# Causal attention on another grid: query chunks of 64 and three times 128, key blocks of 128, with 64x64 corners

## The chip, the cores and the metric

The program runs on one core of one Trainium2 chip. The metric is the device time of the whole program in microseconds (us), the median of three runs. One more execution was recorded by the hardware profiler, and everything below that speaks of engines and waits is read from it.

## What is computed

A causal attention over 2 batches of 12 heads (448 tokens, head size 64), then two MLPs on its 896 x 768 output, the first gated. The weights come as 64-bit floats.

```python
scores = q @ k.T / sqrt(64), masked above the diagonal     # per head, 448 x 448
attn = exp(scores - rowmax); attn /= sum + 1e-9
x = (attn @ v) with the heads side by side                  # 896 x 768
x = (silu(x @ w_gate) * (x @ w_val)) @ w_out                # 768 -> 1536 -> 768
h = x @ w_in                                                # 768 -> 2048
out = (h * clip(h + 3, 0, 6) / 6) @ w2_out                  # 2048 -> 768
```

## The kernel before

The heads are worked in 12 pairs. A pair's q and k lie transposed, head size on the partitions, one head on partitions 0 to 63 and the other on 64 to 127; each is split into a high and a low fp32r part (`qh`, `ql`, `kh`, `kl`). A head's queries and its keys are both cut into four chunks of 112 (`C`, `NC`). Five steps make one pair:

- `sc_parts`: for each chunk c of queries and each head, the three products qh.kh, qh.kl and ql.kh into a PSUM bank (`sc`), 112 rows by (c + 1) x 112 keys (224 at least). A head's contraction is 64 long, so the two heads stand on the two halves of the array's rows and run at the same time. Then VectorE adds the mask and takes the row's maximum (one custom instruction for each chunk, with a read of its accumulator), and ScalarE takes the exponential with its row sum (likewise), into `e`.
- `tp_parts`: TensorE turns every 112x112 block of `e` on or below the diagonal, 20 a pair; six bank copies on ScalarE or VectorE bring them to `et`.
- `pv_parts`, `product`: for each block of keys, `v` (112 x 64, plain f32) times `et`, both heads at the same time on the two halves of the array's columns. An f32 matmul leaves two records in the trace.
- `shares`: the reciprocals of the row sums are spread over 64 columns on GpSimd (`rb`) and turned by TensorE (`tr`), four 112 x 128 transposes.
- `last`: `pv` times the turned reciprocals, and the split of the result for the MLP.

Around them: transfers of q, k and v on SP's queue, turning of q and k (on VectorE from the third pair on, on TensorE for the first two), and near the end the first six-matmul pieces of the MLP (`mm`).

Steps of three pairs are under way at once: at step t the plan is given the scores of pair t, the products with v of pair t - 2 and the transposes of pair t - 1, in this order (`order`). Each step is an `op` with a cost per engine that can take it; `Plan.run` then sets the order on every engine by due times and these costs, and all instructions of the attention are issued from line 74, so that the profile names one line for all and tiles tell them apart. The MLPs behind the attention have a plan of their own, which the change leaves alone.

Of the kernel before, what the change touches and what calls it, by code (L numbers as in the profile page):

```python
# [21 lines left out]
EB = 4  # L22
# [36 lines left out]
GROUPS = ((2,), (0, 1), (3,))  # L59
# [156 lines left out]
def tile_attention_glu_mlp(  # L216
# [38 lines left out]
    OFF = [0, C, 3 * C, 6 * C]  # L255
    KOFF = [0, 4 * C, 7 * C, 9 * C]
    EW = 10 * C
# [77 lines left out]
    def attention():  # L335
        with ExitStack() as st:
# [6 lines left out]
            mask = fix.tile([C, S], F32, name="mask")  # L343
            nc.gpsimd.memset(mask, 0.0)
            nc.gpsimd.affine_select(
                out=mask[:, S - C :], in_=mask[:, S - C :], pattern=[[-1, C]],
                compare_op=ALU.is_ge, fill=LOW, base=0, channel_multiplier=1,
            )
            vset = []
            for i in range(NV):  # L350
                t = fix.tile([C, 2, NC, D + 16], F32, name=f"v1_{i}")
                vset.append(t)
# [183 lines left out]
            def sc_parts(p):  # L536

                if p >= NPAIR:
                    return []
                qh, ql, kh, kl = sets(p)  # L540
                es = e_of[p] = [take("e", EB, [C, EW]) for _ in range(2)]
                ms = [take("m", EB, [C, NC]) for _ in range(2)]
                sm = s_of[p] = take("s", 3, [C, 2, NC])

                def products(group):
                    got = [bank("sc") for _ in range(2)]
                    o, places = 0, {}
                    for c in group:
                        places[c] = o, max(2, c + 1) * C
                        o += places[c][1]  # L550

                    terms = ((qh, kh), (qh, kl), (ql, kh))

                    def work(eng, cs, terms_):
                        for c in cs:
                            o, w = places[c]
# [16 lines left out]
                    for j, (sp, bn) in enumerate(got):  # L573
                        e, m = es[j], ms[j]
                        for x in group:
                            at, w = places[x][0], (x + 1) * C
                            cols_ = slice(OFF[x], OFF[x] + w)
                            op(
                                {"vec": 0.09 + w * 0.00101},
                                lambda eng, x=x, at=at, w=w, cols_=cols_, e=e, m=m, sp=sp: eng.tensor_tensor_reduce(  # L580
                                    out=e()[:, cols_], in0=sp()[:C, at : at + w], in1=mask[:, S - w :], op0=ALU.add,
                                    op1=ALU.min, scale=-SCALE, scalar=3.0e38, accum_out=m()[:, x : x + 1],
                                ),
                                reads=[sp], writes=[(e, x), (m, x)],
                            )
                            op(
                                {"act": 0.28 + w * 0.00083},
                                lambda eng, x=x, cols_=cols_, e=e, m=m, j=j: eng.activation(
                                    out=e()[:, cols_], in_=e()[:, cols_], func=AF.Exp, scale=-1.0, bias=m()[:, x : x + 1],
                                    accum_out=sm()[:, j, x : x + 1],  # L590
                                ),
                                reads=[(m, x)], writes=[(e, x), (sm, (j, x))],
                            )
                        idle.append(bn)

                return [lambda g=g: products(g) for g in GROUPS]

            def tp_parts(p):

                if p < 0 or p >= NPAIR:  # L600
                    return []
                es = e_of.pop(p)
                ets = et_of[p] = [take("et", TB, [C, EW]) for _ in range(2)]

                def turns(j, ks):
# [14 lines left out]
                    n *= C  # L620
                    op(
                        {"act": 0.03 + n * 0.00095, "vec": 0.09 + n * 0.001},
                        lambda eng: move(eng, et()[:, lo : lo + n], tp()[:C, :n]), reads=[tp],
                        writes=[(et, kc) for kc in ks],
                    )
                    idle.append(bn)

                return [lambda j=j, ks=ks: turns(j, ks) for ks in ((0,), (1,), (2, 3)) for j in range(2)]

            def pv_parts(p):  # L630
# [7 lines left out]
                def product(kc):  # L638
                    if kc == 0:
                        box["o"], box["n"] = bank("pv")  # L640
                    o, w = box["o"], (NC - kc) * C

                    def work(eng):
                        for j, et in enumerate(ets):
                            eng.matmul(
                                o()[64 * j : 64 * j + 64, kc * C : S], vt()[:, j, kc, :D], et()[:, KOFF[kc] : KOFF[kc] + w],
                                start=(kc == 0), stop=(kc == NC - 1),
                            )

                    op({"pe": w * 0.0018}, work, reads=[(et, kc) for et in ets] + [vt], writes=[o], kind="pv")  # L650

                def shares():
                    r, rb = take("r", 2, [C, 2, NC]), take("rb", 1, [C, NC, 2, D])
# [9 lines left out]
                        {"pool": 0.72},  # L663
                        lambda e: e.tensor_copy(
                            rb(), r().rearrange("p j c -> p c j").unsqueeze(3).to_broadcast([C, NC, 2, D])
                        ),
# [13 lines left out]
                def last():  # L680
# [961 lines left out]
```

## Time and profile before

| | us |
|---|---|
| median of three runs | 542.94 (541.97 to 543.34) |
| the profiled execution | 542.55 |
| its span, first to last instruction | 540.8 |
| PE / DVE / ACT / POOL busy | 534.3 / 455.9 / 418.6 / 146.2 |

PE is TensorE, PEld its loading of stationary operands, DVE VectorE, ACT ScalarE, POOL GpSimd, SP the queue that issues transfers. The granted clock of TensorE is the full one in all 40 slices of the span. The ends of matmuls in the trace are modelled; their starts are measured, so that a matmul's cost is read from the distance of starts, or from the chain, which counts each piece from the end of the one before. The attention fills the first 92 us.

### The profile page before, as it was taken

To read this page: it belongs to the slowest core of one execution; us is meant where nothing else is said; L and a number is where in the kernel's file an instruction comes from. 1 tells how busy PE (TensorE), PEld (TensorE's weight loads), DVE (VectorE), ACT (ScalarE), POOL (GpSimd) and SP (SyncE) were. 2 spreads that over 40 slices of the span, in tenths; PEclk is the share of its full clock that TensorE was granted. 3 is DMA by queue.
4 is the path that set the end of the run, shared out by engine and by line. 5 is a ranking of instruction groups with operands and counts; after the bars stand their busy time and mean duration, and the time that the engine had idled before them with its cause. 6 is when DMAs were issued, how large, how long until landed. Compare 5 with 4: busy or idle time off the path is not lost.

```text
span 540.8 us, 8943 instructions
## 1 busy us (share of the span) xinstructions
PE 534.3 (99%) x3099; PEld 487.6 (90%) x3099; DVE 455.9 (84%) x931; ACT 418.6 (77%) x877; POOL 146.2 (27%) x163
## 2 busy tenths in 40 slices
PE   8999999999999999999999999999999999999997
PEld 4777777999999999999999999999999999999997
DVE  4999997999878778688998888989888956599982
ACT  5999996878887678588967788899898756686560
POOL 0798988403000000030030143322231300000311
PEclk9999999999999999999999999999999999999999
DMA  7987803355545443332002354465353155510112
GB/s 204 245 215 201 170 17 118 117 180 191 182 148 181 134 135 135 118 116 79 1 1 78 110 176 135 127 185 166 117 163 130 35 180 195 176 58 2 59 45 102
DMA packets 58989, 69.32 MB, mean 128 GB/s; under 512 B 16960, under 2 KB 52544, under 8 KB 58944
## 3 DMA queue, kind: packets, MB, share of 16 engines
q1 hardware_dynamic: 58944, 68.76, 42.4%
q8 instruction: 24, 0.39, 0.3%
q14 instruction: 21, 0.17, 0.1%
HBM read 65.99 MB, written 2.75 MB: 127 GB/s over the span
## 4 chain that ended last, share of the span: by engine, by line
PE 98%; DVE 1%; ACT 0%; issue 0%
PE mm L74 83%; PE pv L74 5%; PE sc L74 4%; PE tp L74 4%; PE tr L74 2%; PE zero L74 1%; DVE out L74 0%; ACT e L74 0%; DVE et L74 0%; ACT qh L74 0%; DVE e L74 0%; DVE zeros L341 0%; DVE half L840 0%; DVE half L839 0%; DVE m L74 0%
## 5 line engine op out<-in xcount | busy, mean ns | idle before, releaser
L74 PE MATMUL mm<-x,a 128*128 128x448 f32 x396 | 85.9, 363 | 0.0
L74 PE MATMUL mm<-x,s 128*128 128x448 f32 x378 | 80.6, 363 | 0.0
L74 PEld LDWEIGHTS mm<-x,a 128*128 128x128 f32 x396 | 74.6, 189 | 5.3
L74 PEld LDWEIGHTS mm<-x,s 128*128 128x128 f32 x378 | 71.2, 188 | 5.1
L74 ACT ACTIVATE raw<-raw,half 128x768 uint32<-128x768 uint8 (+1 forms) x66 | 64.5, 981 | 0.0
L74 PE MATMUL mm<-t,s 128*128 128x448 f32 x270 | 57.8, 363 | 0.0
L74 PE MATMUL mm<-op 128*128 128x384 f32 x315 | 56.5, 336 | 0.0
L74 PEld LDWEIGHTS mm<-op 128*128 128x128 f32 x315 | 55.1, 188 | 0.0
L74 PEld LDWEIGHTS mm<-t,s 128*128 128x128 f32 x270 | 50.7, 188 | 3.7
L74 PE MATMUL mm<-go,wo 128*128 128x448 f32 x252 | 51.2, 363 | 0.0
L74 PEld LDWEIGHTS mm<-go,wo 128*128 128x128 f32 x252 | 47.4, 188 | 3.5 <-issue 0.2
L74 ACT ACTIVATE e<-e,m 112x224 f32<-112x224 f32 (+3 forms) x96 | 49.7, 535 | 0.6 <-DVE m L74 0.6
L74 DVE CUSTOM_DVE_ANT_0 e<-sc,mask 112x224 f32<-112x224 f32 (+3 forms) x96 | 36.6, 440 | 1.2 <-PE sc L74 1.1
L74 DVE SCALAR_TENSOR_TENSOR v<-v,raw 128x768 uint32<-128x768 uint32 x36 | 34.3, 954 | 2.7 <-ACT raw L74 2.4
L74 ACT ACTIVATE w<-raw 128x768 f32<-128x768 f32 (+1 forms) x34 | 29.6, 870 | 8.6 <-DMA raw<-in_moe_w_out_dram 4.3
L74 ACT ACTIVATE v<-raw 128x768 f32<-128x768 f32 x36 | 32.5, 907 | 1.2 <-DMA raw<-in_moe_w_val_dram 1.0
L74 PE MATMUL mm<-x,ws 128*128 128x448 f32 x144 | 30.1, 366 | 0.0
L74 DVE SCALAR_TENSOR_TENSOR w<-w,raw 128x768 uint32<-128x768 uint32 (+1 forms) x30 | 27.2, 906 | 3.0 <-ACT raw L74 3.0
L74 PEld LDWEIGHTS mm<-x,ws 128*128 128x128 f32 x144 | 26.8, 188 | 2.2
L74 ACT COPY tmp<-mm 128x448 f32<-128x448 f32 x40 | 21.2, 532 | 9.0 <-PE mm L74 8.8
L74 ACT CAST op<-h 128x384 fp32r<-128x384 f32 x30 | 15.3, 511 | 16.2 <-PE mm L74 15.5
L74 PE MATMUL tp<-keep,e 112*112 112x112 f32 x240 | 25.8, 260 | 1.4 <-ACT e L74 1.4
(252 smaller groups left out, 1253.6 us busy)
## 6 DMA issues: line engine op xcount, KB each, us to landing
raw<-in_moe_w_out_dram SPq DMA_DIRECT2D x24, 768.0 KB, 4.2
raw<-in_moe_w_in_dram SPq DMA_DIRECT2D x16, 768.0 KB, 4.5
raw<-in_moe_w_gate_dram SPq DMA_DIRECT2D x12, 768.0 KB, 4.2
raw<-in_moe_w_val_dram SPq DMA_DIRECT2D x12, 768.0 KB, 4.2
raw<-in_moe_w_out_dram SPq DMA_DIRECT2D x6, 512.0 KB, 3.4
v<-in_v_dram SPq DMA_DIRECT2D x12, 224.0 KB, 5.1
out_dram<-out SPq DMA_DIRECT2D x14, 192.0 KB, 1.9
nat<-in_k_dram SPq DMA_DIRECT2D x10, 216.0 KB, 4.9
```

Of the source, the lines that this page charges most:

```text
L74: ins = call(*args, **kw)
```

## The change

Queries of a head are cut into chunks of 64, 128, 128 and 128 (`ROWS`), keys into blocks of 128, 128, 128 and 64. Chunk c needs exactly 64, 192, 320 or 448 keys (`WIDE`), and the last block of a chunk's keys is a corner of 64. The chunks of 64 of both heads lie in one tile of 128 partitions, so that the mask, the maximum, the exponential and the row sums take seven passes a pair instead of eight, 1984 columns instead of 2240. Scores go to four banks a pair instead of six, the turned blocks to four instead of six. The products for the chunk of 64 are made in plain f32 with 64 stationary columns. Of `e`, twelve full 128x128 blocks, one 128x64 and six 64x64 corners are turned; `product` has three steps (a 64x64 block, three full ones, three corners); `shares` turns three full blocks and makes two 64x64 products. `v` comes in three transfers a pair instead of one. The plan gets costs for the new pieces.

```diff
...
-GROUPS = ((2,), (0, 1), (3,))
+GROUPS = ((0, 3), (1, 2))
+SMALL, TURN, HALF_TURN, HALF_PV = 0.1, 0.1125, 0.06, 0.13
...
-    OFF = [0, C, 3 * C, 6 * C]
-    KOFF = [0, 4 * C, 7 * C, 9 * C]
-    EW = 10 * C
+    R = S // 7
+    ROWS = [(0, R), (R, 2 * R), (3 * R, 2 * R), (5 * R, 2 * R)]
+    WIDE = [a + n for a, n in ROWS]
+    OFF = [15 * R, 0, 3 * R, 8 * R]
+    EW = 16 * R
+    LONG, MID = ((0, 1), (0, 2), (0, 3), (2, 3)), ((1, 2), (1, 3))
+    HB = 8 * R
...
+            for o, w, r in ((S - 2 * R, 2 * R, slice(0, 128)), (S, R, slice(0, 64)), (S, R, slice(64, 128))):
+                nc.gpsimd.affine_select(
+                    out=mask[r, o : o + w], in_=mask[r, o : o + w], pattern=[[-1, w]],
+                    compare_op=ALU.is_ge, fill=LOW, base=0, channel_multiplier=1,
+                )
...
+                for j in range(2):
+                    op(
+                        {"sp": 0.5},
+                        lambda e, j=j: e.dma_start(
+                            out=vt()[:, j, :3, :D],
+                            in_=v[b, 2 * hp + j, : 6 * R].rearrange("(c p) d -> p c d", p=128),
+                        ),
+                        writes=[(vt, j)], wire=0.43, soon=SOON,
+                    )
                 op(
                     {"sp": 0.5},
                     lambda e: e.dma_start(
-                        out=vt().rearrange("p j c d -> p (j c) d")[:, :, :D],
-                        in_=v[b, 2 * hp : 2 * hp + 2].rearrange("j (c p) d -> p (j c) d", p=C),
+                        out=vt()[:R, :, 3, :D], in_=v[b, 2 * hp : 2 * hp + 2, 6 * R :].rearrange("j p d -> p j d"),
                     ),
-                    writes=[vt], wire=1.0, soon=SOON,
+                    writes=[(vt, 2)], wire=0.15, soon=SOON,
                 )
...
+                        places[c] = o
+                        o += WIDE[c]
...
+                            o, w, (at, n) = places[c], WIDE[c], ROWS[c]
+                            kind = (lambda x: x) if c else (lambda x: x.bitcast(F32))
                             for i in terms_:
                                 a, b = terms[i]
                                 for j, (sp, _) in enumerate(got):
                                     r = slice(64 * j, 64 * j + 64)
+                                    t = sp()[:, o : o + w] if c else got[0][0]()[r, o : o + w]
                                     eng.matmul(
-                                        sp()[:C, o : o + w], a()[r, c * C : (c + 1) * C], b()[r, :w],
-                                        start=(i == 0), stop=(i == 2),
+                                        t, kind(a()[r, at : at + n]), kind(b()[r, :w]), start=(i == 0), stop=(i == 2),
                                     )
...
                     for cs, terms_ in steps:
                         op(
-                            {"pe": len(terms_) * sum(0.005 + places[c][1] * 0.00044 for c in cs)},
+                            {"pe": len(terms_) * sum(max(SMALL, 0.005 + WIDE[c] * 0.00044) if c else HALF_PV for c in cs)},
                             lambda eng, cs=cs, terms_=terms_: work(eng, cs, terms_),
                             reads=[x for i in terms_ for x in terms[i]], writes=[sp for sp, _ in got], kind="sc",
                         )
...
+                            if x == 0 and j:
+                                continue
+                            at, w, n = places[x], WIDE[x], 2 * (x - 1) + j if x else 6
                             cols_ = slice(OFF[x], OFF[x] + w)
+                            low = slice(S - w, S) if x else slice(S, S + R)
...
+                                    out=e()[:, cols_], in0=sp()[:, at : at + w], in1=mask[:, low], op0=ALU.add,
+                                    op1=ALU.min, scale=-SCALE, scalar=3.0e38, accum_out=ms()[:, n : n + 1],
                                 ),
-                                reads=[sp], writes=[(e, x), (m, x)],
+                                reads=[sp], writes=[(e, x), (ms, n)],
...
+                                    out=e()[:, cols_], in_=e()[:, cols_], func=AF.Exp, scale=-1.0, bias=ms()[:, n : n + 1],
+                                    accum_out=sm()[:, n : n + 1],
                                 ),
-                                reads=[(m, x)], writes=[(e, x), (sm, (j, x))],
+                                reads=[(ms, n)], writes=[(e, x), (sm, n)],
...
-                ets = et_of[p] = [take("et", TB, [C, EW]) for _ in range(2)]
-
-                def turns(j, ks):
+                ets = et_of[p] = [take("et", TB, [128, EW]) for _ in range(2)]
+
+                def turns(b):
                     tp, bn = bank("tp")
-                    e, et, lo = es[j], ets[j], KOFF[ks[0]]
+                    et, lo = ets[b // 2], b % 2 * HB
+                    rows, low = slice(0, R if b == 3 else 128), slice(64, 128)
 
                     def work(eng):
-                        for kc in ks:
-                            for c in range(kc, NC):
-                                to = KOFF[kc] - lo + (c - kc) * C
-                                at = OFF[c] + kc * C
-                                eng.transpose(tp()[:C, to : to + C], e()[:, at : at + C], ident[:C, :C])
-
-                    n = sum(NC - kc for kc in ks)
+                        if b == 3:
+                            eng.transpose(tp()[:R, : 2 * R], es[0]()[:, OFF[0] : OFF[0] + R], ident)
+                            for i in range(6):
+                                e, c = es[i // 3], i % 3 + 1
+                                at = OFF[c] + WIDE[c] - R
+                                eng.transpose(
+                                    tp()[:R, (i + 2) * R : (i + 3) * R], e()[low, at : at + R], ident[low, low]
+                                )
+                            return
+                        for i, (j, kc, c) in enumerate(
+                            [(j, *x) for j in range(2) for x in MID] if b == 2 else [(b, *x) for x in LONG]
+                        ):
+                            at = OFF[c] + kc * 128
+                            eng.transpose(tp()[:, i * 128 : (i + 1) * 128], es[j]()[:, at : at + 128], ident)
+
+                    need = [(es[j], c) for j in ((b,) if b < 2 else (0, 1)) for c in ((2, 3) if b == 2 else (1, 2, 3))]
                     op(
-                        {"pe": 0.098 * n}, work, reads=[(e, c) for c in range(ks[0], NC)], writes=[tp], kind="tp",
-                    )
-                    n *= C
+                        {"pe": TURN + 6 * HALF_TURN if b == 3 else 4 * TURN}, work,
+                        reads=need + [(es[0], 0)] * (b == 3), writes=[tp], kind="tp",
+                    )
                     op(
-                        {"act": 0.03 + n * 0.00095, "vec": 0.09 + n * 0.001},
-                        lambda eng: move(eng, et()[:, lo : lo + n], tp()[:C, :n]), reads=[tp],
-                        writes=[(et, kc) for kc in ks],
+                        {"act": 0.03 + HB * 0.00095, "vec": 0.09 + HB * 0.001},
+                        lambda eng: move(eng, et()[rows, lo : lo + HB], tp()[rows]), reads=[tp], writes=[(et, b % 2)],
                     )
                     idle.append(bn)
 
-                return [lambda j=j, ks=ks: turns(j, ks) for ks in ((0,), (1,), (2, 3)) for j in range(2)]
+                return [lambda b=b: turns(b) for b in (0, 1, 3, 2)]
...
-                def product(kc):
-                    if kc == 0:
+                def product(g):
+                    if g == 0:
                         box["o"], box["n"] = bank("pv")
-                    o, w = box["o"], (NC - kc) * C
+                    o = box["o"]
+                    full, low = slice(0, 128), slice(0, 64)
+                    runs = (
+                        (
+                            (low, 0, 0, R, (HB, HB + R), 1), (full, 0, R, 6 * R, (0, HB), 0),
+                            (full, 2, 5 * R, 2 * R, (6 * R, HB + 6 * R), 0),
+                        ),
+                        ((full, 1, 3 * R, 4 * R, (0, 4 * R), 1),),
+                        tuple((low, c, 2 * R * c, R, (HB + (c + 1) * R, HB + (c + 4) * R), 1) for c in (1, 2, 3)),
+                    )[g]
 
                     def work(eng):
-                        for j, et in enumerate(ets):
-                            eng.matmul(
-                                o()[64 * j : 64 * j + 64, kc * C : S], vt()[:, j, kc, :D], et()[:, KOFF[kc] : KOFF[kc] + w],
-                                start=(kc == 0), stop=(kc == NC - 1),
-                            )
-
-                    op({"pe": w * 0.0018}, work, reads=[(et, kc) for et in ets] + [vt], writes=[o], kind="pv")
+                        for rows, kc, to, w, at, i in runs:
+                            for j in range(2):
+                                eng.matmul(
+                                    o()[64 * j : 64 * j + 64, to : to + w], vt()[rows, j, kc, :D],
+                                    ets[i]()[rows, at[j] : at[j] + w], start=kc == 0, stop=True, skip_group_check=True,
+                                )
+
+                    op(
+                        {"pe": sum(HALF_PV if x[3] == R else x[3] * 0.0018 for x in runs)}, work,
+                        reads=[vt] + ([(ets[0], 0), (ets[0], 1), (ets[1], 1)], [(ets[1], 0)], [(ets[1], 1)])[g],
+                        writes=[o], kind="pv",
+                    )
...
                     def work(eng):
-                        for c in range(NC):
+                        for i in range(3):
                             eng.transpose(
-                                tr()[:, c * C : (c + 1) * C], rb()[:, c].rearrange("p j d -> p (j d)"), ident[:C, :C]
+                                tr()[:, R + i * 128 : R + (i + 1) * 128],
+                                rb()[:, 2 * i : 2 * i + 2].rearrange("p j d -> p (j d)"), ident,
                             )
-
-                    op({"pe": 0.4}, work, reads=[rb], writes=[tr], kind="tp")
+                        for j in range(2):
+                            h = slice(64 * j, 64 * j + 64)
+                            eng.matmul(tr()[h, :R], rb()[h, 6], ident[h, h], start=True, stop=True, skip_group_check=True)
+
+                    op({"pe": 3 * TURN + HALF_PV}, work, reads=[rb], writes=[tr], kind="tp")
...
-                return [lambda kc=kc: product(kc) for kc in range(2)] + [shares] + [
-                    lambda kc=kc: product(kc) for kc in range(2, NC)
-                ] + [last]
+                return [lambda: product(0), shares, lambda: product(1), lambda: product(2), last]
...
```

The next two places show PE's own order in the middle of the attention, where the plan repeats it from pair to pair. A row gives the tile written, the tiles read, the size of the output (partitions x columns) and how often the row stands in succession. First, PE from the transposes of one pair (`tp`) into the scores of another (`sc`), before:

```order
L74 MATMUL tp<-keep,e 112x112 x20
L74 MATMUL sc<-kh,qh 112x336 x2
L74 MATMUL sc<-kl,qh 112x336 x2
L74 MATMUL sc<-kh,ql 112x336 x2
L74 MATMUL sc<-kh,qh 112x224 x2
```

and now:

```order
L75 MATMUL tp<-keep,e 128x128 x4
L75 MATMUL sc<-kh,qh 64x64 x2
L75 MATMUL sc<-kl,qh 64x64 x2
L75 MATMUL sc<-kh,ql 64x64 x2
L75 MATMUL sc<-kh,qh 128x448 x2
L75 MATMUL sc<-kl,qh 128x448 x2
```

Between the transposes and the scores with 128 rows now stand the products of the chunk of 64, with 64 rows and 64 columns; the widths 336, 224, 224, 448 became 448, 192 and 320.

Second, PE from the products with v (`pv`) over the turned reciprocals (`tr`) and the transposes (`tp`) to the next scores (`v` with a number is one of its four buffers), before:

```order
L74 MATMUL pv<-et,v_3_95 64x448 x2
L74 MATMUL pv<-et,v_3_95 64x336 x2
L74 MATMUL pv<-et,v_3_95 64x224 x2
L74 MATMUL pv<-et,v_3_95 64x112 x2
L74 MATMUL tr<-keep,rb 128x112 x4
L74 MATMUL tp<-keep,e 112x112 x20
L74 MATMUL sc<-kh,qh 112x336 x2
```

and now:

```order
L75 MATMUL pv<-et,v_2_100 64x64 x2
L75 MATMUL pv<-et,v_2_100 64x384 x2
L75 MATMUL pv<-et,v_2_100 64x128 x2
L75 MATMUL pv<-et,v_2_100 64x256 x2
L75 MATMUL pv<-et,v_2_100 64x64 x6
L75 MATMUL tr<-keep,rb 128x128 x3
L75 MATMUL tr<-keep,rb 64x64 x2
L75 MATMUL tp<-keep,e 128x128 x8
L75 MATMUL tp<-keep,e 64x128
L75 MATMUL tp<-keep,e 64x64 x6
L75 MATMUL tp<-keep,e 128x128 x4
L75 MATMUL sc<-kh,qh 64x64 x2
```

One run of `pv` with 112 keys each, one of `tr` and one of `tp` became: `pv` with 64, with 128 and again with 64 keys; `tr` as three full transposes and two 64x64 products; `tp` as eight full, one with 64 stationary columns, six 64x64 and four full transposes.

## Rows read from the trace of the kernel before

**Rows 1.** The page, busy time and its share of the span, with the number of instructions.

```profile
PE 534.3 (99%) x3099; PEld 487.6 (90%) x3099; DVE 455.9 (84%) x931; ACT 418.6 (77%) x877; POOL 146.2 (27%) x163
```

**Rows 2.** Waits of PE, whole execution: engine, line, waited for: us in total, times, longest.

```profile
PE tp L74 <- ACT e L74: 1.4, 1, 1.4
PE zero L74 <- DVE half L840: 1.2, 1, 1.2
PE sc L74 <- DVE m L74: 0.3, 1, 0.3
```

**Rows 3.** Busy us (instructions) per engine, clock, DMA; seven pairs, one a stretch.

```profile
30.50:36.87 6.37, 6.37 (x65) 4.89 (x64) 6.34 (x24) 6.37 (x25) 5.58 (x9) 1.00 0.97 247
...
68.73:75.11 6.38, 6.38 (x66) 4.90 (x66) 6.26 (x23) 6.31 (x21) 6.15 (x9) 1.00 0.00 0
sum 44.61, PE 44.61 PEld 34.29 DVE 43.47 ACT 44.01 POOL 40.36; mean PE 6.37 PEld 4.90 DVE 6.21 ACT 6.29 POOL 5.77
```

**Rows 4.** The chain, one pair: start us, us, engine, tile, records.

```profile
30.57 1.88 PE sc L74 x24
32.45 2.04 PE pv L74 x16
34.49 0.54 PE tr L74 x4
35.02 1.92 PE tp L74 x20
```

**Rows 5.** The chain, earlier, where v products stand in two pieces.

```profile
17.53 0.90 PE pv L74 x4
...
20.32 1.29 PE pv L74 x12
```

**Rows 6.** The chain, end of the attention: mm is the first MLP matmul.

```profile
83.99 1.41 PE mm L74 x6
85.41 0.38 PE tr L74 x4
85.79 0.77 PE tp L74 x8
86.56 1.23 PE mm L74 x6
```

**Rows 7.** Timeline of PE, one pair's scores: start us, us, stationary partitions*columns, moving operand.

```profile
30.50 0.41 PE L74 MATMUL sc<-kh,qh 64*112 64x336 f32 x2
30.75 0.32 PE L74 MATMUL sc<-kl,qh 64*112 64x336 f32 x2
30.90 0.32 PE L74 MATMUL sc<-kh,ql 64*112 64x336 f32 x2
31.06 0.27 PE L74 MATMUL sc<-kh,qh 64*112 64x224 f32 x2
...
31.68 0.37 PE L74 MATMUL sc<-kh,qh 64*112 64x448 f32 x2
31.88 0.36 PE L74 MATMUL sc<-kl,qh 64*112 64x448 f32 x2
32.09 0.37 PE L74 MATMUL sc<-kh,ql 64*112 64x448 f32 x2
32.38 2.11 PE L74 MATMUL pv<-et,v 112*64 112x448 f32 x16
```

**Rows 8.** Timeline of PE, first transposes of pair 0.

```profile
12.94 0.79 PE L74 MATMUL tp<-keep,e 112*112 112x112 f32 x6 [1.43 <-ACT e L74]
```

**Rows 9.** Timeline, an issue on SP's queue.

```profile
34.17 0.41 SPq L74 DMA_DIRECT2D nat<-in_k_dram  x1
```

**Rows 10.** Groups of instructions by form: busy us, mean ns, idle before; POOL's mask pass.

```profile
L345 POOL TENSOR_SCALAR_AFFINE_SELECT mask<-mask 112x112 f32<-112x112 f32 x1 | 0.3, 278 | 0.0
```

More of the change, by code (lines that the diff above doesn't have):

```diff
@@ L342, in attention @@
             make_identity(nc, ident)
-            mask = fix.tile([C, S], F32, name="mask")
+            mask = fix.tile([128, S + R], F32, name="mask")
             nc.gpsimd.memset(mask, 0.0)
-            nc.gpsimd.affine_select(
-                out=mask[:, S - C :], in_=mask[:, S - C :], pattern=[[-1, C]],
-                compare_op=ALU.is_ge, fill=LOW, base=0, channel_multiplier=1,
-            )
+            for o, w, r in ((S - 2 * R, 2 * R, slice(0, 128)), (S, R, slice(0, 64)), (S, R, slice(64, 128))):
[3 more added lines that the diff above has]
+                )
             vset = []
             for i in range(NV):
-                t = fix.tile([C, 2, NC, D + 16], F32, name=f"v1_{i}")
+                t = fix.tile([128, 2, 4, D + 16], F32, name=f"v1_{i}")
                 vset.append(t)
@@ L540, in sc_parts @@
                 qh, ql, kh, kl = sets(p)
-                es = e_of[p] = [take("e", EB, [C, EW]) for _ in range(2)]
-                ms = [take("m", EB, [C, NC]) for _ in range(2)]
-                sm = s_of[p] = take("s", 3, [C, 2, NC])
+                es = e_of[p] = [take("e", EB, [128, EW]) for _ in range(2)]
+                ms = take("m", 2, [128, 7])
+                sm = s_of[p] = take("s", 3, [128, 7])
                 def products(group):
@@ L548, in products @@
                     for c in group:
-                        places[c] = o, max(2, c + 1) * C
-                        o += places[c][1]
+                        places[c] = o
+                        o += WIDE[c]
                     terms = ((qh, kh), (qh, kl), (ql, kh))
@@ L555, in work @@
                         for c in cs:
-                            o, w = places[c]
+                            o, w, (at, n) = places[c], WIDE[c], ROWS[c]
+                            kind = (lambda x: x) if c else (lambda x: x.bitcast(F32))
                             for i in terms_:
@@ L573, in products @@
                     for j, (sp, bn) in enumerate(got):
-                        e, m = es[j], ms[j]
+                        e = es[j]
                         for x in group:
-                            at, w = places[x][0], (x + 1) * C
+                            if x == 0 and j:
+                                continue
+                            at, w, n = places[x], WIDE[x], 2 * (x - 1) + j if x else 6
                             cols_ = slice(OFF[x], OFF[x] + w)
+                            low = slice(S - w, S) if x else slice(S, S + R)
                             op(
                                 {"vec": 0.09 + w * 0.00101},
-                                lambda eng, x=x, at=at, w=w, cols_=cols_, e=e, m=m, sp=sp: eng.tensor_tensor_reduce(
-                                    out=e()[:, cols_], in0=sp()[:C, at : at + w], in1=mask[:, S - w :], op0=ALU.add,
-                                    op1=ALU.min, scale=-SCALE, scalar=3.0e38, accum_out=m()[:, x : x + 1],
+                                lambda eng, n=n, at=at, w=w, cols_=cols_, e=e, sp=sp, low=low: eng.tensor_tensor_reduce(
+                                    out=e()[:, cols_], in0=sp()[:, at : at + w], in1=mask[:, low], op0=ALU.add,
+                                    op1=ALU.min, scale=-SCALE, scalar=3.0e38, accum_out=ms()[:, n : n + 1],
                                 ),
-                                reads=[sp], writes=[(e, x), (m, x)],
+                                reads=[sp], writes=[(e, x), (ms, n)],
                             )
@@ L587, in products @@
                                 {"act": 0.28 + w * 0.00083},
-                                lambda eng, x=x, cols_=cols_, e=e, m=m, j=j: eng.activation(
-                                    out=e()[:, cols_], in_=e()[:, cols_], func=AF.Exp, scale=-1.0, bias=m()[:, x : x + 1],
-                                    accum_out=sm()[:, j, x : x + 1],
+                                lambda eng, n=n, cols_=cols_, e=e: eng.activation(
+                                    out=e()[:, cols_], in_=e()[:, cols_], func=AF.Exp, scale=-1.0, bias=ms()[:, n : n + 1],
+                                    accum_out=sm()[:, n : n + 1],
                                 ),
-                                reads=[(m, x)], writes=[(e, x), (sm, (j, x))],
+                                reads=[(ms, n)], writes=[(e, x), (sm, n)],
                             )
@@ L636, in pv_parts @@
                 box = {}
-                def product(kc):
-                    if kc == 0:
+                def product(g):
+                    if g == 0:
                         box["o"], box["n"] = bank("pv")
-                    o, w = box["o"], (NC - kc) * C
-                    def work(eng):
-                        for j, et in enumerate(ets):
-                            eng.matmul(
-                                o()[64 * j : 64 * j + 64, kc * C : S], vt()[:, j, kc, :D], et()[:, KOFF[kc] : KOFF[kc] + w],
-                                start=(kc == 0), stop=(kc == NC - 1),
-                            )
-                    op({"pe": w * 0.0018}, work, reads=[(et, kc) for et in ets] + [vt], writes=[o], kind="pv")
+                    o = box["o"]
[8 more added lines that the diff above has]
+                    )[g]
+                    def work(eng):
+                        for rows, kc, to, w, at, i in runs:
[9 more added lines that the diff above has]
+                    )
                 def shares():
-                    r, rb = take("r", 2, [C, 2, NC]), take("rb", 1, [C, NC, 2, D])
+                    r, rb = take("r", 2, [128, 7]), take("rb", 1, [128, 7, D])
                     tr, bn = bank("tr")
@@ L662, in shares @@
                     op(
[L663 to L666, printed above, removed]
+                        {"pool": 0.63},
+                        lambda e: e.tensor_copy(rb(), r().unsqueeze(2).to_broadcast([128, 7, D])),
                         reads=[r], writes=[rb], port=True,
```

## The prediction

> **What bounds the kernel now.** I went from the page to the waits, then to the chain, then to single matmuls. The page has TensorE (PE) busy for 534.3 of 540.8 us [rows 1]; a busy PE can still be a waiting one, so the list of its waits comes next: over the whole execution it waited 1.4 us once for a softmax result, 1.2 us at the very start and 0.3 us once [rows 2]. Everything else is PE running one matmul behind the other. The change touches only the attention, the first 92 us. There seven head pairs in a row take 6.36 to 6.38 us each; of those 6.37 us PE is busy all 6.37, ScalarE (ACT) 6.29 and VectorE (DVE) 6.21 [rows 3]. Three engines look full, and the question is which sets the period. A period set by ACT or DVE would show PE gaps; there are none. So an instruction saved on ACT or DVE is worth nothing here, and PE's time per pair is worth twelve times itself, since PE has no slack behind the attention either.
>
> The chain splits a period: scores 1.88, products with v 2.04, spreading of the reciprocals 0.54, transposes 1.92, in all 6.38 [rows 4]. What these contain is the second thing to read. A matmul uses the whole array, half of its rows (at most 64 partitions of contraction), half of its columns (at most 64 stationary columns), or a quarter. The same work costs more when the piece before it had another shape:
> - four `tr` transposes take 0.54 after `pv` (half columns to whole array) [rows 4], and 0.38 after `mm` (whole to whole) [rows 6]: 0.16 for the change of shape;
> - the sixteen `pv` records take 2.04 in one piece [rows 4], and 0.90 + 1.29 = 2.19 where the scores of the next pair were put between them [rows 5]: 0.15 for one more entry;
> - six `mm` take 1.41 after `pv` and 1.23 after `tp` [rows 6]: 0.18;
> - scores: steps of 0.155 at 336 columns, 0.62 for six of 224, 0.205 at 448 [rows 7], so 3 x 0.155 + 0.62 + 3 x 0.205 = 1.70 for the matmuls, and 1.88 - 1.70 = 0.18 for entering from the transposes.
>
> Another data type alone costs nothing: `mm` (fp32r) and the f32 transposes follow each other on the whole array without it [rows 6]. A pair of before has three changes of shape (into sc, pv, tr): 0.18 + 0.15 + 0.16 = 0.49, and 5.89 us of matmuls.
>
> **The change part by part.** *Matmuls.* Scores: three terms at 448 columns stay 0.615; 320 columns lie between 224 and 336, by proportion 0.148, three are 0.44; 192 columns lie between 0.088 (by columns from 448) and 0.103 (the 224 step), I take 0.10, three are 0.30; the shared 64 chunk runs in plain f32 on quarters, both heads side by side. Its price comes from `pv`, f32 too: 2.04 - 0.15 = 1.89 us for 448 + 336 + 224 + 112 = 1120 columns, 1.69 ns a column, 0.108 for 64, three are 0.32. Sum 1.68 against 1.70. `pv`: 384 + 128 + 256 + 4 x 64 = 1024 columns, 1.73 against 1.89. `tp`: 1.92 / 20 = 0.096 for 112 columns [rows 4], so 0.110 for 128 and 0.055 for 64; thirteen with 128 and six with 64 make 1.76 against 1.92. `tr`: 3 x 0.110 + 0.108 = 0.44 against 0.38. In all 5.61 against 5.89: 0.28 less a pair, **-3.4 us** for twelve. Rounding in these proportions leaves 1 us to either side.
>
> *Changes of shape.* A pair of after goes: quarter, half rows (scores); quarter, half columns, quarter (pv); whole, quarter (tr); whole, half columns, quarter, whole (tp). That is eleven changes for three. Over the whole program, counted in its order, 135 for 47: 88 more. No row of before shows a quarter of the array, so the price there is bounded by the four above, 0.15 to 0.18, above, and by nothing at all, below. The dear two load 112 or 128 fp32r columns after the change, the cheap ones 64 columns or transposes; the new ones are nearly all 64 wide or transposes. I take the nearest row, 0.15: 88 x 0.15 = **+13.2 us**. At 0.12 it is 10.6, at 0.18 it is 15.8.
>
> The Trainium skill (TensorEngine Tiling (Array Packing), Key Properties) says that a change of tiling mode, not of the tile alone, drains TensorE. The rows above show drains for four pairs of shapes; the rule would make every one of the 88 pay, quarters included, and so stands with the +13.2 and not with the first two rivals below.
>
> *ACT and DVE.* Seven exponentials and seven max passes a pair instead of eight, four bank copies instead of six, 1984 and 2048 columns instead of 2240: both get lighter, below a period that they don't set, and I count 0. Where it can count is the start, before the pipeline is full: the first transposes of pair 0 wait 1.43 us for their exponentials [rows 8]. The new first transposes need three chunks of one head, behind four exponentials on ACT where the old ones stood behind five. All of it gone is -1.4, none of it, with the new entries in the first scores, +0.5; I take **-0.5**.
>
> *SP, POOL, DMA.* v comes in three transfers for one, two more issues of 0.41 us a pair on SP's queue [rows 9], for the same bytes, ahead of the next q and k; PE waited for no transfer anywhere [rows 2], and with a longer period there is more room. Two more mask passes of at most 0.28 us on POOL [rows 10] end before the first scores. Both 0; if v came late, `pv` of pair 0 would wait once, well under 1 us.
>
> *Sum:* 13.2 - 3.4 - 0.5 = +9.3 on the profiled execution's 542.55: 551.9. That execution lies 0.4 under the median 542.94, so **552** against the median.
>
> **The rivals.**
> - *Only entering or leaving the whole array costs* (a quarter is reached from a half for nothing). 74 such changes for 36, +38 x 0.15 = 5.7, less 3.9: +1.8, 544.7. For it: no row shows a quarter. Against it: scores to pv is half rows to half columns, and pays 0.15.
> - *The price belongs to the change of step, not of shape*, so changes inside a step are free: 0 - 3.4 - 0.5, **539.0**, faster. It decides from the point where the mean price of the added changes falls below 3.9 / 88 = 0.044. For it: in before each change of shape is also one of step. Against it: tr to tp, tp to mm and mm to tr are changes of step too, and their 0.38 and 1.23 hold no such price [rows 6].
> - *The quarters don't run side by side.* The two heads' 64x64 products come from different halves of the rows into one bank, which nothing in before does. One after the other they cost 4 x 0.108 = 0.43 more a pair, +5.2: 557.4.
> - *The seven small transposes a pair take twice as long*, because a piece with half the columns is not transposed the fast way: 6 x 0.055 + 0.110 = 0.44 a pair, +5.3: 557.5. For it: `tp` at 0.096 for 112 columns takes half of what `pv` takes, 1.69 x 112 = 0.19, so there is a fast way. Against it: nothing here. The Trainium skill (same page, Restrictions) has transpose mode for f32 disabled under column tiling; by it this rival would hold, and no row of before can show it.
>
> **How the numbers follow.** Forecast 0.62, its own range 547.5 to 557 (price 0.12 to 0.18, the matmuls 1 us either way, the start -1.4 to +0.5). Whole-array rival 0.14, step rival 0.10, the two slower ones together 0.14. What this kernel's measurement can tell from no change is 0.3%, 1.6 us: 541.3 to 544.6. Below lie the step rival and 0.01 of the whole-array rival: 0.11. Within lie 0.06 of the whole-array rival and 0.05 of the forecast, where quarters cost a fraction: 0.11. Above lies the rest: 0.78. The range for 8 in 10 leaves out the step rival and the far end of the slower ones: 543.5 to 558.5.
>
> **What would show it.** The chain's pieces in a steady pair: sc near 2.0, pv 2.2, tr 0.75, tp 2.35, period 7.3, with PE still without gaps; ACT and DVE at 0.8 to 0.85 of it. A step from the third to the fourth `pv` piece, or into the six small transposes, of 0.15 more than the columns explain confirms the price; a step of just the columns takes it away. Small `sc` products of the two heads starting together refute the third rival, small transposes at 0.055 the fourth. The forecast is wrong at its root if the period stays under 6.5, or if PE waits in the attention.

## The result, and the profile after

The changed kernel takes 550.58 us (median of 4 runs, 550.25 to 550.75) where the kernel before, run beside it, takes 542.65 (541.97 to 543.34): a ratio of 1.0145, 95% interval 1.0133 to 1.0157. The forecast was 552.0, slower.

The page, and the waits of PE over the whole execution, as in [rows 1, 2]:

```profile
PE 541.9 (99%) x3339; PEld 492.4 (90%) x3339; DVE 452.3 (82%) x898; ACT 415.6 (76%) x841; POOL 142.5 (26%) x162
```

```profile
PE tp L75 <- ACT e L75: 1.3, 1, 1.3
PE zero L75 <- DVE half L881: 1.2, 1, 1.2
PE tr L75 <- DMA nat<-in_k_dram: 0.2, 1, 0.2
```

PE is busy 7.6 us longer, VectorE 3.6 and ScalarE 3.0 less, and PE still waits nowhere in the attention after its start. Four pairs, one to a stretch, as in [rows 3]:

```profile
31.32:38.52 7.20, 7.20 (x87) 5.33 (x88) 6.20 (x21) 6.59 (x21) 5.59 (x8) 1.00 0.68 188
...
sum 28.77, PE 28.77 PEld 21.29 DVE 24.22 ACT 25.16 POOL 22.89; mean PE 7.19 PEld 5.32 DVE 6.05 ACT 6.29 POOL 5.72
```

A pair takes 7.19 us for 6.37 and PE is busy in all of it. VectorE is busy for 0.84 of a pair and ScalarE for 0.87; ScalarE's 6.29 us are as many as before. The chain, one pair, for [rows 4]; then the end of the attention, for [rows 6]:

```profile
38.52 2.08 PE sc L75 x29
40.60 2.20 PE pv L75 x28
42.80 0.74 PE tr L75 x7
43.54 2.17 PE tp L75 x19
```

```profile
88.38 1.22 PE mm L75 x6
89.60 2.02 PE tp L75 x19
91.62 0.59 PE tr L75 x7
92.21 1.41 PE mm L75 x6
...
100.27 24.83 PE mm L75 x122
```

Each of the four pieces is longer than before: +0.20, +0.16, +0.20, +0.25. At the end the price is seen by itself: `tr` takes 0.59 where it follows `tp`, whole array on whole array, and 0.74 where it follows `pv`; six `mm` take 1.22 after a `tp` that ends on the whole array and 1.41 after a `tr` that ends on quarters. The attention's last `pv` or `tr` ends at 100.27 us; in the chain of before the last piece of the attention ended here:

```profile
90.55 2.04 PE pv L74 x16
92.59 32.51 PE mm L74 x160
```

The difference, 7.68 us, is all of the 7.70 between the two profiled executions (550.25 and 542.55): the MLPs behind didn't change. The scores of one pair in PE's timeline from the second small term on, for [rows 7] (stationary partitions*columns, then the moving operand):

```profile
38.61 0.28 PE L75 MATMUL sc<-kl,qh 64*64 64x64 f32 x4
38.73 0.28 PE L75 MATMUL sc<-kh,ql 64*64 64x64 f32 x4
38.94 0.47 PE L75 MATMUL sc<-kh,qh 64*128 64x448 f32 x2
39.25 0.37 PE L75 MATMUL sc<-kl,qh 64*128 64x448 f32 x2
39.46 0.37 PE L75 MATMUL sc<-kh,ql 64*128 64x448 f32 x2
```

Read the distances of starts. From the second to the third small term is 0.12 for four records, two heads by two f32 passes: the quarters of the two heads run side by side (one after the other, the forecast had 0.22). The last small term takes 0.21 to the first half-row matmul, 0.09 more than its columns, and that one takes 0.31 to the next, 0.10 more than the 0.20 of a steady step: the new shape costs time ahead of its first matmul and again behind it.

For [rows 8] and [rows 9], the first wait for a softmax (PE's timeline) and the transfers of v on SP's queue; the two new passes over the mask [rows 10] take POOL 0.23 us each.

```profile
12.28 0.55 PE L75 MATMUL tp<-keep,e 128*128 128x128 f32 x3 [1.29 <-ACT e L75]
```

```profile
34.85 2.33 SPq L75 DMA_DIRECT2D v<-in_v_dram  x3
```

Three issues of v hold SP's queue for 2.33 us, nearly twice the 0.41 each of the forecast, and PE waits for none of them. The first transposes begin 0.66 us earlier (12.28 for 12.94), and their wait for the softmax is only 0.14 shorter. That the change makes them earlier is not shown: e1_scatter below has the same instructions up to there, and they begin at 13.19 in its profile:

```profile
13.19 0.55 PE L75 MATMUL tp<-keep,e 128*128 128x128 f32 x3 [1.29 <-ACT e L75]
```

The wait is the same 1.29 us; already the first scores are 0.91 later (7.82 for 6.91). By so much the opening differs from one profiled execution to another.

### The profile page after: what moved, and what is told of

It is laid out like the page before. It is cut to its first block, busy times and chain, and to the rows that moved or that the text cites. A ratio compares the mean times of both kernels' runs of the same rounds, so it can differ in the third digit from the quotient of the medians.

```text
span 548.4 us, 9380 instructions
## 1 busy us (share of the span) xinstructions
PE 541.9 (99%) x3339; PEld 492.4 (90%) x3339; DVE 452.3 (82%) x898; ACT 415.6 (76%) x841; POOL 142.5 (26%) x162
## 4 chain that ended last, share of the span: by engine, by line
PE 97%; ACT 1%; DMA 1%; DVE 0%; SPq 0%; issue 0%
PE mm L75 81%; PE pv L75 5%; PE sc L75 5%; PE tp L75 5%; PE tr L75 2%; DMA nat<-in_k_dram 1%; SPq L75 0%; DVE out L75 0%; ACT e L75 0%; ACT et L75 0%; ACT qh L75 0%; DVE e L75 0%; DVE m L75 0%
## 5 line engine op out<-in xcount | busy, mean ns | idle before, releaser
L75 ACT ACTIVATE e<-e,m 128x320 f32<-128x320 f32 (+3 forms) x84 | 43.8, 523 | 2.7 <-DVE m L75 2.3
L75 DVE CUSTOM_DVE_ANT_0 e<-sc,mask 128x192 f32<-128x192 f32 (+3 forms) x84 | 32.4, 447 | 5.5 <-PE sc L75 5.2
L75 PE MATMUL tp<-keep,e 128*128 128x128 f32 (+2 forms) x228 | 27.4, 262 | 1.4 <-ACT e L75 1.3
```

Of the source, the lines that this page charges most:

```text
L75: ins = call(*args, **kw)
```

## The experiments

Theory: PE pays about 0.15 us whenever one matmul uses another part of the array than the one before, and this price alone makes the kernel slower. Rivals: the small pieces are themselves dear; some shapes count as one; ScalarE or VectorE sets the period. The first four kernels keep every matmul of the changed kernel and change only the order; the kernel before took 542.65 us beside them.

**More changes, the same matmuls** (`e1_scatter`). Each 64x64 block of `pv` is put behind another full one.

```diff
+        (low, 1, 2 * R, R, (HB + 2 * R, HB + 5 * R), 1),
+    ),
+    (
         (full, 2, 5 * R, 2 * R, (6 * R, HB + 6 * R), 0),
+        (low, 2, 4 * R, R, (HB + 3 * R, HB + 6 * R), 1),
     ),
-    ((full, 1, 3 * R, 4 * R, (0, 4 * R), 1),),
-    tuple((low, c, 2 * R * c, R, (HB + (c + 1) * R, HB + (c + 4) * R), 1) for c in (1, 2, 3)),
+    ((full, 1, 3 * R, 4 * R, (0, 4 * R), 1), (low, 3, 6 * R, R, (HB + 4 * R, HB + 7 * R), 1)),
...
```

> The same matmuls as in the changed kernel (550.6 us), but the three 64x64 corners of the products with v stand each behind another full block, so that the array changes between half columns and quarter seven times a pair in pv instead of three. Counted over the program, 42 changes of shape more. Theory (each change of shape costs about 0.148 us, as the changed kernel's trace shows): +6.2 us, 556.8; pv 2.20 -> about 2.79 in the chain. Rival (the price belongs to the change of step, changes inside a step are free or hidden): 550.6. Rival (small pieces are dear by themselves): 550.6, since their number is the same.

557.07 us (556.69 to 557.49), ratio 1.0268 (1.0253 to 1.0282). The chain, `pv` of one pair:

```profile
42.99 2.79 PE pv L75 x28
```

The same 28 records take 2.79 for 2.20: four entries, 0.148 each. This is the price with nothing else changed. A pair takes 7.79.

**Quarters of `pv` and `tr` joined** (`e2_pv_tr`): `pv` makes its 64x64 blocks last and `tr` its two 64x64 products first.

```diff
-        (low, 0, 0, R, (HB, HB + R), 1), (full, 0, R, 6 * R, (0, HB), 0),
-        (full, 2, 5 * R, 2 * R, (6 * R, HB + 6 * R), 0),
+        (full, 0, R, 6 * R, (0, HB), 0), (full, 2, 5 * R, 2 * R, (6 * R, HB + 6 * R), 0),
...
-    tuple((low, c, 2 * R * c, R, (HB + (c + 1) * R, HB + (c + 4) * R), 1) for c in (1, 2, 3)),
+    (
+        *((low, c, 2 * R * c, R, (HB + (c + 1) * R, HB + (c + 4) * R), 1) for c in (1, 2, 3)),
+        (low, 0, 0, R, (HB, HB + R), 1),
+    ),
...
+    for j in range(2):
+        h = slice(64 * j, 64 * j + 64)
+        eng.matmul(tr()[h, :R], rb()[h, 6], ident[h, h], start=True, stop=True, skip_group_check=True)
     for i in range(3):
...
-    for j in range(2):
-        h = slice(64 * j, 64 * j + 64)
-        eng.matmul(tr()[h, :R], rb()[h, 6], ident[h, h], start=True, stop=True, skip_group_check=True)
```

> The same matmuls as in the changed kernel, but in pv all 64x64 products come last, and in tr the two 64x64 products come first, next to them. 28 changes of shape fewer over the program (two to three a pair). Theory: -4.1 us, 546.5; pv about 2.05 and tr about 0.6 in the chain. Rivals (price of a step, or small pieces dear by themselves): 550.6.

547.36 us (546.04 to 548.45: two runs near 546.2, two near 548.4), ratio 1.0087 (1.0068 to 1.0106). The two longer ones show a mean granted clock of 0.996, the other two 0.999 and 1.00; beside the latter, 546.5 was right. A pair takes 6.75, from one start of `sc` to the next in the chain:

```profile
37.20 2.08 PE sc L75 x29
...
43.95 2.08 PE sc L75 x29
```

**Small transposes last** (`e3_tp`).

```diff
-    return [lambda b=b: turns(b) for b in (0, 1, 3, 2)]
+    return [lambda b=b: turns(b) for b in (0, 1, 2, 3)]
```

> The same matmuls as in the changed kernel, but the six small transposes of a pair come last in tp, right before the 64x64 score products of the next pair. 19 changes of shape fewer, 8 of them because small transposes and 64x64 products follow each other. Theory, if those two count as one shape: -2.8 us, 547.8; if a small transpose and a 64x64 product are two shapes: about -1.6, 549.0. Rival (price of a step): 550.6.

549.46 us (549.03 to 551.03), ratio 1.0132 (1.0118 to 1.0146). `tp` loses 0.15, `sc` nothing:

```profile
38.40 2.07 PE sc L75 x30
40.47 2.20 PE pv L75 x28
42.67 0.74 PE tr L75 x7
43.41 2.02 PE tp L75 x19
```

So a 64x64 transpose and a 64x64 product are two shapes, though the trace writes 64*64 for both.

**All three orders together** (`e4_grouped`: the edits of e2_pv_tr and e3_tp).

> Both regroupings together: whole array, quarter, half rows, half columns, quarter, and whole again, five changes a pair instead of ten, 43 fewer over the program. Theory: -6.3 us against the changed kernel, 544.3 and so still 1.6 above before (542.65). Rival (small pieces dear by themselves, or price of a step): 550.6.

545.45 us (544.92 to 545.83), ratio 1.0054 (1.004 to 1.0068). A pair takes 6.59:

```profile
36.42 2.07 PE sc L75 x30
...
43.01 2.08 PE sc L75 x30
```

Of the 0.82 us a pair, 0.60 is gone with no matmul taken away. The 544.3 expected counted a small transpose and a 64x64 product as one shape; as two, which e3_tp shows, 35 changes are gone and not 43, and 35 x 0.148 = 5.2 us gives 545.4, as measured.

**Half-row scores first** (`e5_quarter_last`, on e4_grouped).

```diff
-GROUPS = ((0, 3), (1, 2))
+GROUPS = ((1, 2), (3, 0))
```

> The version with all three orders grouped (545.45 us), with the scores of the half-row chunks first and those of the shared 64 last. The small transposes then stand right ahead of the half-row scores (64 rows by 128 columns of the array) and the 64x64 scores right ahead of the half-column products with v; the count of changes between shapes is the same. If the small transposes count as a shape of their own, the order is worth nothing: 545.4 us, sc still near 2.08 in the chain. If they count as the shape of the half-row scores, one entry of 0.20 us a pair goes: 12 x 0.20 = 2.4 us less, 543.0 us, sc near 1.88.

545.33 us (544.62 to 547.72), ratio 1.0058 (1.004 to 1.0077). By the time it is the first case, by the trace nearer the second: a pair takes 6.45, 0.14 less. PE's timeline where the small transposes meet the half-row scores:

```profile
50.59 0.35 PE L75 MATMUL sc<-kh,qh 64*128 64x192 f32 x1
50.64 0.33 PE L75 MATMUL tp<-keep,e 64*64 64x64 f32 x3
```

The first head's scores (upper half of the rows) start before the last three small transposes (lower half): there is no gap between the two at all. Twelve times 0.14 does not show in the time. The profile tells where one execution lost it. Windows of this kernel, columns as in [rows 3], the granted clock third from the end:

```profile
9.00:12.00 3.00, 2.02 (x19) 1.20 (x18) 2.06 (x10) 2.00 (x7) 0.00 (x0) 1.00 0.81 213
12.00:15.00 3.00, 2.67 (x28) 2.04 (x30) 2.86 (x9) 2.09 (x9) 0.78 (x2) 0.91 0.85 261
15.00:18.00 3.00, 3.00 (x17) 2.66 (x15) 1.47 (x8) 1.80 (x6) 2.26 (x3) 0.52 0.44 94
```

After a stretch in which PE was busy 2.02 of 3 us and waited 1.1 for a softmax, the granted clock falls to 0.52, nearly the whole stretch at the lower level of 1.2 GHz, and PE gets through 17 records in 3 us. The same windows of e4_grouped, the first and the last:

```profile
9.00:12.00 3.00, 1.78 (x14) 1.00 (x13) 2.81 (x13) 2.47 (x9) 0.00 (x0) 1.00 0.77 198
15.00:18.00 3.00, 3.00 (x37) 2.25 (x35) 3.00 (x13) 2.88 (x8) 2.81 (x4) 1.00 0.52 120
```

There PE had been busy for less, 1.78 of 3 us, its wait was 1.3, and the clock stayed at 1.00: what made it fall is open. The fall is not the whole loss. In the MLP a run of `mm` begins at 120.16 us where e4_grouped begins it at 120.42, so the time lost by the fall had been won back. Then PE waits for ScalarE, which had waited 1.45 us for a transfer of weights, and the next such run begins at 126.46 for 125.86:

```profile
124.55 2.07 PE L75 MATMUL mm<-t,s 128*128 128x448 f32 x9 [0.60 <-ACT mm L75]
```

Of the six executions timed, three with a mean granted clock of 0.998 to 1.00 took 544.62 to 544.75, and three with 0.993 to 0.997 took 545.9 to 547.72.

**The same from the second pair on** (`e9_quarter_last_later`).

```diff
-    return [lambda g=g: products(g) for g in GROUPS]
+    return [lambda g=g: products(g) for g in (GROUPS if p > 0 else ((0, 3), (1, 2)))]
```

> The half-row scores first, as in e5_quarter_last, but from the second pair on; the first pair keeps the order of the grouped version. In e5_quarter_last a pair took 6.44 us against 6.59, yet the time was only 0.1 us lower: between 15 and 18 us its granted clock fell to 0.52, after a wait of 1.1 us for the first softmax. If that start ate the gain, the clock stays at 1.00 here and pairs take 6.44: counted with a transpose as wide as the array whatever its columns, there are 81 changes of shape against 89 of the grouped version, 8 x 0.14 = 1.1 us less, 544.3 us. If the shorter pairs are worth nothing in the end, 545.4 us. If something other than the start lost it, the pairs are at 6.44 with the clock at 1.00 and the time is still 545 or above.

544.94 us (544.65 to 545.3), ratio 1.0039 (1.0026 to 1.0053), the kernel before at 542.97. The clock is 1.00 in the whole attention and pairs take 6.45, but the time lies between the two cases, near what e5_quarter_last takes at the full clock. The planner also put the last three pairs in another order, and in the one execution profiled the third pair's scores begin 0.85 us later than in e4_grouped (18.33 for 17.48), as much as openings differ. That a fall of the clock cost e5_quarter_last time is shown by its windows; what else keeps both kernels above their forecasts is not shown beyond this.

**Quarters joined across pairs** (`e6_quarters_joined`): the 64x64 scores of a pair are issued among the 64x64 products with v of the pair two before (`first_` makes the scores of p + 2, `work` the products of p).

```diff
-GROUPS = ((0, 3), (1, 2))
+GROUPS = ((3,), (1, 2))
...
+    late[p] = lambda: products((0,))
...
+    if g == 2 and p + 2 in late:
+        rest = late.pop(p + 2)()
+        next(rest)
+        first_, more_r, more_w = joined.pop()
+        parts = [first_, work]
```

> The grouped version, with the 64x64 scores of a pair issued among the 64x64 products with v of the pair two before, from the third pair on: one entry into the 64x64 shape and one out of it go in ten pairs, and over the whole program 72 changes of shape (without the free step to the 64-column transposes) stand against 81 of the grouped version. By 0.15 to 0.18 us each that is 1.4 to 1.6 us less than 545.45: 543.9 us if the small transposes are a shape of their own. If they count as the shape of the half-row scores that now follow them, 10 x 0.20 = 2.0 us more goes: 541.9 us. If moving the scores makes their softmax late, waits of the transposes on ScalarE appear in the chain (tp<-ACT e) and the time is 546 us or above.

542.17 us (541.62 to 543.01, 11 runs) beside 542.63 (23 runs): ratio 0.9989 (0.998 to 0.9998). One pair of the chain:

```profile
49.59 1.44 PE sc L75 x14
51.02 1.45 PE pv L75 x12
52.47 0.43 PE sc L75 x9
...
52.96 0.40 PE pv L75 x14
...
53.42 0.59 PE tr L75 x6
54.02 1.71 PE tp L75 x16
```

6.30 us, below the 6.37 of before, and the second case of its expectation within 0.3. It is the fastest kernel of the study, but half a microsecond is inside what this kernel's measurement can tell from no change.

**A lighter ScalarE in the kernel before** (`e8_before_act_light`).

```diff
+def thin(x, c):
+    return slice(c.stop - C, c.stop) if x == 3 else c
...
-    out=e()[:, cols_], in_=e()[:, cols_], func=AF.Exp, scale=-1.0, bias=m()[:, x : x + 1],
+    out=e()[:, thin(x, cols_)], in_=e()[:, thin(x, cols_)], func=AF.Exp, scale=-1.0, bias=m()[:, x : x + 1],
```

> The kernel before, with the exponential of the longest chunk taken over its last 112 columns alone; the 336 columns before them are left without it, so the softmax of that chunk isn't computed. ScalarE loses about 0.3 us in each of 24 instructions (0.70 to 0.41 us), 0.6 us a pair and 7 us in all; TensorE's instructions are the same. If TensorE alone sets the pace, as the prediction has it, the time stays at 542.65 us within 0.6. If ScalarE, busy for 6.29 of a pair's 6.37 us, paced the pairs as well, a pair falls towards TensorE's own length or below and the time goes down by several us, to about 536.

542.22 us (541.78 to 543.47), ratio 0.9994 (0.9986 to 1.0003). Three pairs of it:

```profile
sum 19.11, PE 19.11 PEld 14.68 DVE 18.17 ACT 17.36 POOL 16.75; mean PE 6.37 PEld 4.89 DVE 6.06 ACT 5.79 POOL 5.58
```

ScalarE has 0.5 us less a pair than in [rows 3], the period is 6.37 as before: an engine busy for 6.29 of 6.37 us had set nothing. The third pair's scores begin at 17.66 in this chain, 18.43 in that of before. Of these 0.77 us the first transposes' wait for ScalarE is 0.28 (1.15 for 1.43); 0.51 is there at the first scores (6.80 for 7.31), ahead of every exponential.

## Why the prediction was right

The versions side by side. Changes of shape in a steady pair are counted in the programs, a transpose counted as wide as the array whatever its columns; periods are from the chain.

| version | changes a pair | period | 5.69 + 0.15 each | time |
|---|---|---|---|---|
| e1_scatter | 14 | 7.79 | 7.79 | 557.07 |
| the changed kernel | 10 | 7.19 | 7.19 | 550.58 |
| e3_tp | 9 | 7.03 | 7.04 | 549.46 |
| e2_pv_tr | 7 | 6.75 | 6.74 | 547.36 |
| e4_grouped | 6 | 6.59 | 6.59 | 545.45 |
| e5_quarter_last, e9_quarter_last_later | 5 | 6.45, 6.45 | 6.44 | 545.33, 544.94 |
| e6_quarters_joined | 4 | 6.30 | 6.29 | 542.17 |

Seven orders of the same matmuls lie on one line to 0.01 us; 5.69 is what the line leaves for the matmuls alone. That is the mechanism of the forecast, with its price: 0.15. Two things were settled after the runs: the line's two numbers are fitted, and the rule for transposes was taken from the changed kernel, e3_tp and e5_quarter_last. The price is a mean: it is 0.148 in e1_scatter, and 0.09 + 0.10 around the first half-row scores of the changed kernel.

- *Matmuls.* 5.69 us a pair against the 5.61 forecast, so 0.20 less than before's 5.89 and not 0.28: -2.4 us for twelve where -3.4 stood.
- *Changes.* The price of 0.15 held, the count didn't: the eleventh change of a pair, from the whole transposes into the 128x64 one, is free, so that 77 more of them pay and not 88: +11.5 us for +13.2. Four narrow windows of PE's timeline of the changed kernel, each with the start of its first record:

```profile
36.98 0.49 PE L75 MATMUL tp<-keep,e 128*128 128x128 f32 x3
```

```profile
37.20 0.45 PE L75 MATMUL tp<-keep,e 128*64 128x128 f32 x2
```

```profile
37.41 0.30 PE L75 MATMUL tp<-keep,e 64*64 64x64 f32 x2
```

```profile
37.65 0.53 PE L75 MATMUL tp<-keep,e 64*64 64x64 f32 x3
```

  The first row's three start at 36.98, 37.09 and 37.20, the third being the 128x64 one: 0.11 from the one before, its columns and nothing more. To the first 64x64 transpose it is 0.21 for the same columns: about 0.10 ahead of it for that change, where the prediction asked for 0.15. Between 37.41 and 37.65 lie four steps of small transposes, 0.06 each. So `tp` took 2.17 where 2.35 stood; `pv` at 2.20 (2.2) and `tr` at 0.74 (0.75) came as forecast, `sc` 0.08 above its 2.0, and the period is 7.19 instead of 7.3.
- *Start.* -0.5 stood here. 11.5 - 2.4 is 9.1, and 7.7 was measured: -1.4 is left for it, the far end of its range; that is a remainder and not a measurement. In the chain the third pair's scores begin 0.37 us ahead of before, in spite of the changes paid by then, and the ten rounds from there lose 8.05:

```profile
18.06 2.09 PE sc L75 x30
```

  In before that piece began at 18.43. A wait of 0.3 for a maximum is gone [rows 2]. The first transposes stand 0.66 earlier, but e1_scatter, with the opening of the changed kernel, has them 0.25 later than the kernel before: that the change makes the start cheaper is not shown, and the cause of the -1.4 stays open.
- *The sum.* +9.3 stood there: eleven changes too many (1.7), a saving of the matmuls 1.0 too large, and a start 0.9 too dear, by the remainder above. That the terms missed in both directions is luck in the sum's favour.
- *ACT, DVE, SP, POOL at nothing:* right; e8_before_act_light shows it for ACT in the kernel before, the list of waits for the others. That ACT gets lighter in a steady pair was wrong: 6.29 us before and after.
- *The rivals.* That only the whole array costs: refuted by e1_scatter, where quarters and half columns alternate at 0.148. That the step costs and not the shape: refuted by the same run, which has as many steps as the changed kernel and three of its four new changes within one. That the quarters don't run side by side: refuted by the 0.12 of the small scores. That small transposes take twice as long: refuted by their 0.06.

The Trainium skill (TensorEngine Tiling (Array Packing), Key Properties) has a change of tiling mode drain TensorE; the rows agree that it costs, 0.15 us in the mean. They show the price and not the draining. The same page (Restrictions) has transpose mode for f32 switched off under column tiling. No run shows a slow transpose; the free step into the 128x64 one, the free step from 64x64 transposes to half-row scores and the paid one to 64x64 products all fit transposes that use the full width of the array however few their columns are.

## What to carry to other kernels

Where TensorE has no gaps, count how often successive matmuls change the part of the array they use, before counting the columns a finer grid saves: here 77 more changes cost more than four times what the smaller blocks gave back. If the finer grid is wanted, issue pieces of one shape together, across steps and across pairs; that alone took back 8.4 us. An engine that is busy 99% of a period need not set it: look for gaps of the bottleneck.

## What was not expected

- A transpose of 64 columns goes with the wide shapes: no price after 128x128 transposes (0.11 from start to start) and none before half-row products on the other half of the rows, which even start ahead of the last small transposes (50.59 and 50.64 us).
- The Trainium skill (TensorEngine Tiling (Array Packing), Restrictions and Gotchas) says that different row tiles can't use one PSUM bank at the same time. Here the 64x64 scores of both heads, from the two halves of the rows, go to one bank, four records in 0.12 us: side by side. The measurement decides.
- In one execution of e5_quarter_last 1.1 us of waiting was followed by about 3 us at a granted clock of 0.52; e4_grouped waited 1.3 us and kept the full clock.
- The opening of the program, up to the first transposes, ended 0.91 us apart in two profiled executions with the same instructions; differences of that size between versions can't be read from single profiles.
